# Last expert without products between its pieces, earlier decoding of the first dense columns, another use of a spare buffer: a fused attention, mixture and dense kernel

## The chip, the core and the metric

The kernel runs on one core of one Trainium2 chip. The metric is the time of one execution on the device in microseconds (us); the times below are medians of runs. The trace is of one further, profiled execution. Its engines are TensorE (PE, with its weight loads shown apart as PEld), VectorE (DVE), ScalarE (ACT), GpSimd (POOL) and SyncE (SP); here SP alone issues the loads from and stores to main memory, which 16 DMA engines carry out.

## What is computed

Three layers follow one another on 2304 tokens of width 512 (4 batches of 576; float32, the dense weights come as 64-bit floats):

```python
# attention, 8 heads of 64: heads 0-3 see the 32 latest positions, heads 4-7 every 32nd
attn = softmax(where(mask, scale * q @ k.T, -1e9));  x = attn @ v          # x: 2304 x 512
# mixture: 8 experts with 4 slots each, 512 -> 1024 -> 512
logits = x @ phi                                      # 2304 x 32
slot_input = softmax(logits, axis=0).T @ x            # 32 x 512
h = maximum(slot_input[e] @ w1[e], 0);  slot_out[e] = h @ w2[e]
x = softmax(logits, axis=1) @ slot_out                # 2304 x 512
# dense layer, 512 -> 2048 -> 512
h = x @ w_in;  g = where(h > 0, h, exp(minimum(h, 0)) - 1)
out = g @ w_out
```

## The kernel before

**Stages.** First comes the attention: 20 units (`units`, the loop over `it` at L498), each a head pair `p`, a stretch `t` and a half `h`, in the order of pairs 2, 3, 0, 1. While it runs, the first-layer weights `w1[e]` of the experts are loaded, 2 MB each in four DMAs of 512 KB. Then the column softmax and its product (`acc`, L574) give the 32 slot inputs. `emit_w1(a)` (L658) makes the first expert layer for two experts at a time, `a` from 0 to 3, `emit_w2(e)` (L748) the second layer, eight products for each expert, all added up in one place (`acc`; the variable is `yp`). Each of the eight takes 32 columns of the PE array; the eight go round its four column groups twice. The eight experts' results are 32 rows. Copies (`y_sb`, L800 on ACT and L801 on DVE), products with a 0/1 matrix (L805), the copy `soT` (L807) and products with the dense weight (L883, L894) turn them into a small matrix `M4`, so that the wide product with `w_in` over all tokens is one with `M4` and the row softmax `cT` (L974). From there the dense stage runs: exponential and the like on ACT and DVE, and three products for each 128 tokens and 128 rows of `w_out` (L1016 to L1018), since both sides are split in a high and a low part.

**Decoding.** A dense weight is stored as a 64-bit float. `dec_abs` (L727, ACT) and `dec_1`, `dec_2`, `dec_3` (L731, L735, L741, DVE) turn one block of it into 32-bit floats. The first 256 columns of `w_in` are loaded early as four "heads" of 256 KB, each behind an expert's weight in the spare end of its buffer (`load_head`, L450). Decoded they go to `dec`, which is the buffer half `wb0`. That half holds the second expert's `w2` until that expert's products are done.

**Buffers and loads.** The weights lie in regions that the attention uses first: slot 9 is `kA` (the keys of pairs 2 and 0), slot 7 is `kB` (pairs 3 and 1), slot 5 the queries of pairs 3 and 0, slot 6 the values of pair 0, slots 1, 2 and 4 other regions of the attention. Slot 8 (`ex`) belongs to nothing else. The table `LOADS` (L489) says behind which unit which `w1` is issued into which slot. `load_w` issues a weight; L703 issues the second-layer weights `w2[3]` to `w2[7]` behind `emit_w1(a)`. All loads stand in one row on SP. Each of them waits for the load eight places ahead of it to have landed, and for the last reader of its buffer; what stands behind a waiting load waits with it. Behind the experts come `w_out` for the first blocks (L722, into `wb1`), the other 256 columns of the first `w_in` block (L716, slot 9), and further blocks of both.

**Warm-up products.** `warm(n)` (L411) emits 2n products of a matrix with itself whose result nobody reads. `W6` is how many stand between the pieces of the last expert (L752), `W7` and `W8` those around L805. In the dense stage's first microseconds a planner (L1062 on) works out an order of all remaining instructions from estimated durations; where it expects PE to be idle, it fills in such products (L1111), as many as its estimate gives.

Of the kernel before, what the change touches and what calls it, by code (L numbers as in the profile page):

```python
# [19 lines left out]
def attn_moe_mlp(ctx, tc, q, k, v_l, v_s, phi, w1, w2, w_in, w_out, out):  # L20
# [12 lines left out]
    NEG = -8.0e9  # L33
    SLOT = 4608
    W0, W2, W3, W4, W5 = 8, (0, 0, 0, 0, 0), 0, 0, 0
    W6, W7, W8, W9 = 1, 3, 2, 1
    CO = (2, 3, 0, 1)
    Q0, WC = 4, 4
    HALF = S * B
# [17 lines left out]
    WP, HP = 256, 2  # L57
# [17 lines left out]
    def slot(i, name):  # L75
        if not isinstance(i, int):
            return i
        t = region(SLOT_AT[i], name)
        return t[:, 0:min(SLOT, t.shape[1])]
# [272 lines left out]
    with tc.manual_schedule():  # L352
# [92 lines left out]
        wsl, w_tiles, w64h = {}, {}, []  # L445
# [7 lines left out]
        def load_w(e, second, s, part=None):  # L453
            if (e, second) not in wsl:

                if not isinstance(s, int):
                    t = s
                elif second:
                    t = w_tiles[s]
                else:  # L460
                    t = w_tiles[s] = slot(s, f"w{e}")
                t = t[:, 0:4096]
                wsl[e, second] = t.rearrange("p (c x) -> p c x", c=8 if second else 4)
            t = wsl[e, second]
            src = w2[e].rearrange("c p x -> p c x") if second else w1[e].rearrange("(c p) x -> p c x", p=128)
            if not second:
                for c in range(4):
                    nc.sync.dma_start(out=t[:, c], in_=src[:, c])
                if s in (9, 5, 7):
                    load_head(s)  # L470
                return
            for c in range(0, 8, 2) if part is None else range(part, part + 4, 2):
                nc.sync.dma_start(out=t[:, c:c + 2].rearrange("p c x -> p (c x)"), in_=src[:, c // 2])
# [6 lines left out]
        def qkv(p, kind):  # L480
# [7 lines left out]

        LOADS = {  # L489
            0: ((0, "q"), (0, "v")), 3: ((0, "k"), (0, 0), (1, "q")), 5: ((1, "v"),), 7: ((1, "k"),),  # L490
            9: ((1, 2), (2, 4)), 13: ((3, 9), (4, 5)), 15: ((5, 8), (6, 6)), 19: ((7, 7),),
        }

        nu = len(units)
# [159 lines left out]
        def emit_w1(a):  # L654
            hp = s_ps[a % 2]
            for c in CO:
                for g in range(4):
                    nc.tensor.matmul(  # L658
                        hp[32 * g:32 * g + 32, :], siT[:, c, :], w_at(2 * a + g // 2, 0, 2 * c + g % 2),
                        start=(c == CO[0]), stop=(c == CO[-1]),  # L660
                    )
            hs = small("pt", 512, "hs", 2)
            nc.scalar.activation(out=hs, in_=hp, func=AF.Relu)
            return hs

        def emit_h1T(a, hs):
            ps = ps_t.tile([128, 4, 4, NS], F32, tag="t", name="htps")
            for c in range(4):
                nc.tensor.transpose(
                    ps[:, c].rearrange("p g s -> p (g s)"), hs[:, 128 * c:128 * c + 128], ident  # L670
                )
            for e2 in range(2):
                e = 2 * a + e2
                nc.vector.tensor_copy(
                    out=h1T[e][:, :, SPE * e:SPE * e + SPE].rearrange("p (f c) s -> p f c s", f=2),
                    in_=ps[:, :, 2 * e2:2 * e2 + 2, SPE * e:SPE * e + SPE].rearrange("p c f s -> p f c s"),
                )
# [14 lines left out]
        for a in range(NE // 2):  # L692
            hs = emit_w1(a)
            if a == 0:
                nc.scalar.activation(out=c4[:, :, 0, :].bitcast(F32R), in_=lt, func=AF.Copy)
                nc.vector.tensor_tensor(out=c4[:, :, 2, :], in0=lt, in1=c4[:, :, 0, :], op=ALU.subtract)
                for x in (0, 2):
                    nc.scalar.activation(out=c4[:, :, x + 1, :], in_=c4[:, :, x, :], func=AF.Copy)
            if prev is not None:
                emit_h1T(*prev)  # L700
            prev = (a, hs)
            for e, x in (((3, 0), (4, 2)), ((5, 4),), ((6, 5), (7, 8)), ())[a]:
                load_w(e, 1, x)  # L703

        w64 = {}
# [1 line left out]
        def load_w64(kind, i, s, part=None):  # L707
            if (kind, i) not in w64:
                t = slot(s, f"w64_{kind}_{i}")[:, 0:4096]
                w64[kind, i] = t.rearrange("p (c x a) -> p c x a", c=4, a=2).bitcast(I32)  # L710
            t = w64[kind, i].rearrange("p c x a -> p c (x a)")
            if kind == 0:
                src = w_in[:, 1024 * i:1024 * i + 1024].rearrange("(c p) f -> p c f", p=128)
                if part is not None:
                    t, src = t[:, :, 2 * part[0]:2 * part[1]], src[:, :, 2 * part[0]:2 * part[1]]
                nc.sync.dma_start(out=t, in_=src)  # L716
            else:
                src = w_out[512 * i:512 * i + 512, :].rearrange("(c p) x -> p c x", p=128)
                if part is None:
                    nc.sync.dma_start(out=t, in_=src)  # L720
                else:
                    nc.sync.dma_start(out=t[:, part], in_=src[:, part])  # L722
# [3 lines left out]
        def dec_abs(src, dst):  # L726
            nc.scalar.activation(out=dst, in_=src[:, :, 1].bitcast(F32), func=AF.Abs, scale=ESC)  # L727
# [17 lines left out]
        def emit_w2(e):  # L745
            for c in range(8):
                g = c % 4
                nc.tensor.matmul(  # L748
                    yp[32 * g:32 * g + 32, :], h1T[e][:, c, :], w_at(e, 1, c),
                    start=(e == 0 and c < 4), stop=(e == NE - 1 and c >= 4),  # L750
                )
                if e == NE - 1 and c in (1, 3, 5):  # L752
                    warm(W6)

        pers = slot(6, "pers")
        dec = wb0.rearrange("p (i x) -> p i x", x=512)
# [13 lines left out]
        for e in range(NE - 1):  # L770
            emit_w2(e)
            if e == 1:
                emit_h1T(*prev)
            if e >= 4:
                for i0 in range(6 * (e - 4), 6 * (e - 4) + 6, 3):
                    emit_ct(i0)
        for c in range(4):
            dec_abs(w64h[c], dec[:, c, 0:WP])
        for c in range(4):
            for d_ in (dec_1, dec_2, dec_3):  # L780
                d_(w64h[c], dec[:, c, 0:WP])
        warm(W5)
        emit_w2(NE - 1)
        loads, due = {}, -1.35
# [9 lines left out]
            due += 5.83  # L794
            loads[x] = due
        load_w64(0, 1, 0)
        load_w64(1, 1, 5)

        y_sb = small("pt", DM, "y_sb", 2)
        nc.scalar.activation(out=y_sb[:, 0:256], in_=yp[:, 0:256], func=AF.Copy)  # L800
# [234 lines left out]
        for si, gi, s, f0, f1, y, T in ev_n:  # L1035
# [18 lines left out]
            x = node("V" if f0 else "A", 0.6 if f0 else 0.48, deps, key, f_ev, ("ob", rel) if f1 == NF else None)  # L1054
# [30 lines left out]
        while len(order) < len(nodes):  # L1085
            best = (1e8,)
            for e in free:
                c = [(start_of(n), nodes[n][3], n) for n in ready[e]]
                if c:
                    lim = min(c)[0] + EPS  # L1090
                    x = min((key, t, n) for t, key, n in c if t <= lim)
                    best = min(best, (x[1], x[2], e))
            t, n, e = best
# [72 lines left out]
```

## Time and profile before

| | us |
|---|---|
| median of 3 runs | 378.37 |
| lowest and highest of them | 377.45, 378.55 |
| the profiled execution | 376.64 |
| its span, first to last instruction | 374.9 |

In the span PE is busy 341.6 us (91%), PEld 249.6 us, DVE 255.8 us, ACT 233.9 us, POOL 35.1 us. The span falls into an attention up to some 92 us, a mixture up to some 144 us, and the dense stage from 150.64 us, when the first L1016 starts. The profile gives start, duration and count of instructions in order of time, with the idle time ahead of them and what ended it in brackets; a row can stand for several instructions of one kind. Matmuls overlap, so that the starts of successive rows say more than the durations. The DMA rows give the time from the issue of a load to its landing.

### The profile page before, as it was taken

How to read it: one execution, taken by the hardware profiler on the slowest of the kernel's cores; microseconds unless marked ns; L12 is line 12 of the kernel's file. 1: busy time of each engine (PE TensorE's matmuls, PEld its weight loads, DVE VectorE, ACT ScalarE, POOL GpSimd, SP SyncE). 2: the span in 40 equal slices, each digit the busy share in tenths (PEclk: the TensorE clock that was granted, in tenths of full speed). 3: DMA queues.
4: the chain of work that ended last, by engine and by line, in shares of the span. 5: the costliest groups of instructions: out<-in, count | busy, mean ns of one | idle time of the engine just before them, and what ended most of it. 6: DMA issues, size and time to landing. Idle time of an engine off the chain costs nothing.

```text
span 374.9 us, 8089 instructions
## 1 busy us (share of the span) xinstructions
PE 341.6 (91%) x3287; PEld 249.6 (67%) x3287; DVE 255.8 (68%) x522; ACT 233.9 (62%) x462; POOL 35.1 (9%) x75
## 2 busy tenths in 40 slices
PE   6365988878799999999999999999999999999995
PEld 4344666556233337878688778888868888888884
DVE  6564858658360028979999999999854665476741
ACT  6395865325232046999999678868665666666660
POOL 8401964000020000000000000000000000000000
PEclk9598899989999999999999999999999999999999
DMA  6999999998999989764100144100000011032301
GB/s 205 394 399 392 395 331 366 379 407 319 388 412 406 408 352 379 294 226 166 59 2 0 27 200 169 55 3 0 0 2 0 0 57 57 0 114 112 113 2 57
DMA packets 23606, 71.64 MB, mean 191 GB/s; under 512 B 2192, under 2 KB 2320, under 8 KB 23568
## 3 DMA queue, kind: packets, MB, share of 16 engines
q1 hardware_dynamic: 23568, 71.12, 49.9%
q8 instruction: 26, 0.43, 0.5%
q14 instruction: 12, 0.10, 0.1%
HBM read 66.39 MB, written 4.72 MB: 190 GB/s over the span
## 4 chain that ended last, share of the span: by engine, by line
PE 83%; ACT 6%; DVE 4%; issue 3%; DMA 2%; SPq 0%; ACTq 0%
PE ops L1016 18%; PE ops L1017 17%; PE ops L1018 17%; PE hps L974 4%; PE acc L748 4%; PE s_ps L658 4%; ACT bd L258 2%; DMA kA<-in_k_dram 2%; PE xtps L334 2%; PE s_ps L200 2%; PE lo L292 2%; PE so L316 1%; PE wps L1111 1%; PE acc L574 1%; PE ptps L272 1%
## 5 line engine op out<-in xcount | busy, mean ns | idle before, releaser
L984 DVE SCALAR_TENSOR_TENSOR g<-hps,g 128x512 f32<-128x512 f32 (+1 forms) x80 | 50.6, 632 | 18.2 <-ACT g L981 18.2
L978 ACT ACTIVATE g<-hps 128x512 f32<-128x512 f32 (+1 forms) x80 | 44.2, 552 | 20.6 <-PE hps L974 19.2
L981 ACT ACTIVATE g<-g 128x512 f32<-128x512 f32 (+1 forms) x80 | 46.9, 586 | 1.4
L1018 PE MATMUL ops<-wh,glo 128*128 128x512 f32 x86 | 33.5, 390 | 0.0
L1018 PE MATMUL ops<-w,glo 128*128 128x512 f32 x86 | 33.5, 389 | 0.0
L990 ACT ACTIVATE ghi<-g 128x512 fp32r<-128x512 f32 (+1 forms) x40 | 23.5, 588 | 14.3 <-DVE g L984 12.9
L990 ACT ACTIVATE rings<-g 128x512 fp32r<-128x512 f32 (+1 forms) x40 | 23.4, 586 | 13.2 <-DVE g L984 11.1
L974 PE MATMUL hps<-pers 128*128 128x512 f32 (+1 forms) x80 | 29.3, 372 | 0.0
L1016 PE MATMUL ops<-wh,ghi 128*128 128x512 f32 x72 | 28.9, 401 | 0.0
L1016 PE MATMUL ops<-wh,rings 128*128 128x512 f32 x72 | 28.8, 400 | 0.0
L1016 PE MATMUL ops<-w,ghi 128*128 128x512 f32 x72 | 28.5, 395 | 0.0
L1017 PE MATMUL ops<-wl,ghi 128*128 128x512 f32 x72 | 28.1, 390 | 0.0
L1017 PE MATMUL ops<-w,rings 128*128 128x512 f32 x72 | 28.1, 390 | 0.0
L1016 PE MATMUL ops<-w,rings 128*128 128x512 f32 x72 | 28.1, 390 | 0.0
L1017 PE MATMUL ops<-w,ghi 128*128 128x512 f32 x72 | 28.1, 390 | 0.0
L1017 PE MATMUL ops<-wl,rings 128*128 128x512 f32 x72 | 28.0, 390 | 0.0
L523 POOL COPY v<-v 32x768 f32<-32x768 f32 (+2 forms) x28 | 20.6, 743 | 26.0 <-DMA v<-in_v_l_dram 21.9
L1018 PE MATMUL ops<-wh,rings 128*128 128x512 f32 x58 | 22.6, 390 | 0.0
L731 DVE TENSOR_SCALAR xw<-xw 128x512 int32<-128x512 int32 (+1 forms) x36 | 13.7, 389 | 13.0 <-ACT xw L727 12.9
L1018 PE MATMUL ops<-w,rings 128*128 128x512 f32 x58 | 22.6, 389 | 0.0
L225 DVE TENSOR_REDUCE mx<-s_ps 128x6 f32<-128x384 f32 (+1 forms) x20 | 10.2, 509 | 15.2 <-PE s_ps L214 9.2
L994 DVE TENSOR_TENSOR glo<-g,rings 128x512 fp32r<-128x512 f32 (+1 forms) x24 | 15.2, 632 | 7.2 <-ACT rings L990 5.0
(193 smaller groups left out, 712.3 us busy)
## 6 DMA issues: line engine op xcount, KB each, us to landing
w<-in_moe_w_dram SPq DMA_DIRECT2D x52, 512.0 KB, 9.3
w<-in_moe_w_in_dram SPq DMA_DIRECT2D x3, 2048.0 KB, 8.6
out_dram<-ob SPq DMA_DIRECT2D x18, 256.0 KB, 2.0
v<-in_v_s_dram SPq DMA_DIRECT2D x8, 512.0 KB, 8.7
xw<-in_moe_w_dram SPq DMA_DIRECT2D x8, 512.0 KB, 9.6
xw<-in_moe_w_out_dram SPq DMA_DIRECT2D x2, 2048.0 KB, 7.8
q<-in_q_dram SPq DMA_DIRECT2D x7, 576.0 KB, 9.6
kB<-in_k_dram SPq DMA_DIRECT2D x8, 288.0 KB, 8.8
```

Of the source, the lines that this page charges most:

```text
L523: nc.gpsimd.tensor_copy(out=o, in_=i)
L658: nc.tensor.matmul(hp[32 * g:32 * g + 32, :], siT[:, c, :], w_at(2 * a + g // 2, 0, 2 * c + g % 2), start=(c == CO[0]), stop=(c == CO[-1]),)
L748: nc.tensor.matmul(yp[32 * g:32 * g + 32, :], h1T[e][:, c, :], w_at(e, 1, c), start=(e == 0 and c < 4), stop=(e == NE - 1 and c >= 4),)
L974: nc.tensor.matmul(t["ps"], M4[:, 128 * f:128 * f + 128], cTf[:, t0:t0 + n], start=True, stop=True)
L978: nc.scalar.activation(out=t["g"], in_=t["ps"], func=AF.Exp)
L981: nc.scalar.activation(out=t["g"], in_=t["g"], func=AF.Relu, scale=-1.0, bias=1.0)
L984: nc.vector.scalar_tensor_tensor(out=t["g"], in0=t["ps"], scalar=0.0, in1=t["g"], op0=ALU.max, op1=ALU.subtract)
L990: nc.scalar.activation(out=t["hi"], in_=t["g"], func=AF.Copy)
L994: nc.vector.tensor_tensor(out=t["lo"], in0=t["g"], in1=t["hi"].bitcast(F32), op=ALU.subtract)
L1016: nc.tensor.matmul(o, t["hi"][:, c], hi, start=(f == f0), stop=False)
L1017: nc.tensor.matmul(o, t["hi"][:, c], lo, start=False, stop=False)
L1018: nc.tensor.matmul(o, t["lo"][:, c], hi, start=False, stop=(f == f1 - 1))
```

## The change

Three edits, in their code:

```diff
-    W6, W7, W8, W9 = 1, 3, 2, 1
+    W6, W7, W8, W9 = 0, 3, 2, 1
...
         LOADS = {
             0: ((0, "q"), (0, "v")), 3: ((0, "k"), (0, 0), (1, "q")), 5: ((1, "v"),), 7: ((1, "k"),),
-            9: ((1, 2), (2, 4)), 13: ((3, 9), (4, 5)), 15: ((5, 8), (6, 6)), 19: ((7, 7),),
+            9: ((1, 2), (2, 4), (3, 8)), 13: ((4, 9), (5, 5)), 15: ((6, 6),), 19: ((7, 7),),
...
-            for e, x in (((3, 0), (4, 2)), ((5, 4),), ((6, 5), (7, 8)), ())[a]:
+            for e, x in (((3, 0), (4, 2)), ((5, 4), (6, 8)), ((7, 5),), ())[a]:
                 load_w(e, 1, x)
...
             if e == 1:
                 emit_h1T(*prev)
+                for c in range(4):
+                    dec_abs(w64h[c], dec[:, c, 0:WP])
+                for c in range(4):
+                    for d_ in (dec_1, dec_2, dec_3):
+                        d_(w64h[c], dec[:, c, 0:WP])
             if e >= 4:
                 for i0 in range(6 * (e - 4), 6 * (e - 4) + 6, 3):
                     emit_ct(i0)
-        for c in range(4):
-            dec_abs(w64h[c], dec[:, c, 0:WP])
-        for c in range(4):
-            for d_ in (dec_1, dec_2, dec_3):
-                d_(w64h[c], dec[:, c, 0:WP])
...
-        load_w64(1, 1, 5)
+        load_w64(1, 1, 8)
```

On PE the last expert's products stand like this before (`w_1338` is that expert's `w2`, x2 are two of its eight products; L416 are the warm-up products):

```order
L764 MATMUL ctps<-ident,c_1823 128x128 x6
L748 MATMUL acc<-w_1338,h1T_c 32x512 x2
L416 LDWEIGHTS ident
L416 MATMUL wps<-ident 128x256
L416 LDWEIGHTS ident
L416 MATMUL wps<-ident 128x256
L748 MATMUL acc<-w_1338,h1T_c 32x512 x2
L416 LDWEIGHTS ident
L416 MATMUL wps<-ident 128x256
L416 LDWEIGHTS ident
L416 MATMUL wps<-ident 128x256
L748 MATMUL acc<-w_1338,h1T_c 32x512 x2
```

and like this after, where the buffer is called `w_1200`:

```order
L748 MATMUL acc<-w_901,h1T_b 32x512 x8
L764 MATMUL ctps<-ident,c_1823 128x128 x6
L748 MATMUL acc<-w_906,h1T_b 32x512 x8
L764 MATMUL ctps<-ident,c_1823 128x128 x6
L748 MATMUL acc<-w_1200,h1T_c 32x512 x8
L416 LDWEIGHTS ident
L416 MATMUL wps<-ident 128x256
```

The eight products now stand in one row; six warm-up products are gone, and nothing else on PE has moved.

On ACT, between the ReLU of the first expert layer (L663) and the copy of the result (L800), the four decoding steps (L727) change places with the six copies of the row softmax (L765):

```order
 L663 ACTIVATE hs<-s_ps_91 128x512
 L663 ACTIVATE hs<-s_ps_92 128x512
-L765 ACTIVATE pers<-ctps 128x3x4x32 x6
-L727 ACTIVATE xw<-w_1189 128x256
-L727 ACTIVATE xw<-w_1195 128x256
+L727 ACTIVATE xw<-w_1194 128x256
+L727 ACTIVATE xw<-w_1200 128x256
 L727 ACTIVATE xw<-w_1607 128x256
 L727 ACTIVATE xw<-w1s 128x256
+L765 ACTIVATE pers<-ctps 128x3x4x32 x6
 L800 ACTIVATE y_sb<-acc 128x256
```

On DVE the twelve decoding steps have no instruction between their old place and their new one, so that DVE's row reads as before.

On SP, in the attention's second half, the loads behind the third expert's `w1` (`w_901`) before (`w_1189` is the fourth expert's, in slot 9):

```order
L468 DMA w_901<-in_moe_w_dram 128x1024 [waits DMAHW3_49]
L468 DMA w_1189<-in_moe_w_dram 128x1024 [waits DMAHW4_49,PE_49]
L468 DMA w_1189<-in_moe_w_dram 128x1024 [waits DMAHW5_49]
L468 DMA w_1189<-in_moe_w_dram 128x1024 [waits DMAHW6_49]
L468 DMA w_1189<-in_moe_w_dram 128x1024 [waits DMAHW7_49]
L450 DMA w_1189<-in_moe_w_in_dram 128x512 [waits DMAHW0_49]
```

and after (`w_906` is the fourth expert's, in slot 8; `w_1194` the fifth's, in slot 9):

```order
L468 DMA w_901<-in_moe_w_dram 128x1024 [waits DMAHW3_49]
L468 DMA w_906<-in_moe_w_dram 128x1024 [waits DMAHW4_49]
L468 DMA w_906<-in_moe_w_dram 128x1024 [waits DMAHW5_49]
L468 DMA w_906<-in_moe_w_dram 128x1024 [waits DMAHW6_49]
L468 DMA w_906<-in_moe_w_dram 128x1024 [waits DMAHW7_49]
L468 DMA w_1194<-in_moe_w_dram 128x1024 [waits DMAHW0_49,PE_49]
```

The fourth expert's weight no longer waits for PE, only for the load eight places ahead (the DMAHW names); the wait for PE now stands at the fifth expert's weight, `w_1194`. The number of loads on SP and their order by expert are as before; the two early heads of `w_in` go with the fifth and the sixth expert's weight instead of the fourth and the fifth. The planner's order for the dense stage is the same.

## Rows read from the trace of the kernel before

**Rows 1.** The page: PE's granted clock in 40 slices of the span, in tenths.

```profile
PEclk9598899989999999999999999999999999999999
```

**Rows 2.** Windows: start:end length, busy of each engine, PEclk, DMA share, GB/s.

```profile
150.00:160.00 10.00, 10.00 (x47) 8.11 (x45) 10.00 (x25) 9.99 (x22) 0.00 (x0) 1.00 0.69 273
...
360.00:370.00 10.00, 10.00 (x46) 8.28 (x45) 2.86 (x8) 3.06 (x8) 0.00 (x0) 1.00 0.01 2
```

**Rows 3.** Timeline of PE, seventh and eighth expert to the dense stage.

```profile
134.38 1.92 PE L748 MATMUL acc<-w,h1T_b 128*32 128x512 f32 x16
136.24 0.88 PE L764 MATMUL ctps<-ident,c 128*128 128x128 f32 x6
137.04 1.05 PE L748 MATMUL acc<-w,h1T_c 128*32 128x512 f32 x4
...
140.96 1.05 PE L748 MATMUL acc<-w,h1T_c 128*32 128x512 f32 x4
141.95 0.83 PE L416 MATMUL wps<-ident 128*128 128x256 bf16 x6
...
150.64 0.48 PE L1016 MATMUL ops<-wh,rings 128*128 128x512 f32 x1
```

**Rows 4.** Timeline of SP's issues, and each one's KB and us to landing.

```profile
127.46 0.33 SPq L473 DMA_DIRECT2D w<-in_moe_w_dram  x1
...
128.75 0.33 SPq L473 DMA_DIRECT2D w<-in_moe_w_dram  x1
...
w<-in_moe_w_dram SPq DMA_DIRECT2D x1, 512.0 KB, 10.2
...
130.07 0.33 SPq L722 DMA_DIRECT2D xw<-in_moe_w_out_dram  x1
...
xw<-in_moe_w_out_dram SPq DMA_DIRECT2D x1, 512.0 KB, 10.1
...
139.32 0.38 SPq L716 DMA_DIRECT2D w<-in_moe_w_in_dram  x1
```

**Rows 5.** Windows, as in rows 2: the load stream full, and its gaps.

```profile
62.00:64.00 2.00, 1.81 (x66) 1.34 (x55) 1.61 (x5) 1.14 (x3) 0.00 (x0) 1.00 0.65 219
86.00:87.00 1.00, 1.00 (x60) 0.69 (x50) 0.92 (x4) 0.13 (x1) 0.00 (x0) 1.00 0.52 197
130.00:135.00 5.00, 5.00 (x48) 2.07 (x44) 0.00 (x0) 1.71 (x4) 0.00 (x0) 1.00 1.02 406
```

**Rows 6.** SP's longest wait between 80 and 95 us, and the issue behind it.

```profile
SPq L468 <- PE lg L341: 7.8, 1, 7.8
...
86.55 1.02 SPq L468 DMA_DIRECT2D w<-in_moe_w_dram  x2
```

**Rows 7.** Timeline of ACT and DVE around the decoding and behind it.

```profile
131.55 0.87 ACT L765 ACTIVATE pers<-ctps 128x384 fp32r<-128x384 f32 x2 [9.87 <-PE ctps L764]
...
142.12 0.39 ACT L800 ACTIVATE y_sb<-acc 128x256 f32<-128x256 f32 x1 [3.13 <-PE acc L748]
142.40 0.67 ACT L727 ACTIVATE xw<-xw 128x512 f32<-128x512 f32 x1
...
138.05 0.29 DVE L731 TENSOR_SCALAR xw<-xw 128x256 int32<-128x256 int32 x1 [12.02 <-ACT xw L727]
...
142.54 0.42 DVE L801 COPY y_sb<-acc 128x256 f32<-128x256 f32 x1
```

**Rows 8.** Timeline of PE at two stops, windows behind and between, the code queue.

```profile
15.48 0.76 PE L214 MATMUL s_ps<-kA,q 128*18 128x36 f32 x37 [6.02 <-DMA kA<-in_k_dram]
...
77.91 0.30 PE L292 MATMUL lo<-v,lpt 64*32 64x64 f32 x3 [2.31 <-issue]
...
78.00:82.00 4.00, 4.00 (x87) 2.70 (x87) 2.48 (x7) 0.49 (x1) 0.00 (x0) 0.57 1.03 411
100.00:102.00 2.00, 1.06 (x6) 0.14 (x4) 0.76 (x2) 0.31 (x1) 0.00 (x0) 1.00 1.03 411
...
q8 instruction: 26, 0.43, 0.5%
```

## The prediction

> **What bounds the kernel now.** I read the timeline of PE from the end. From the first L1016 at 150.64 us on, each stretch of 10 us up to 370 us shows PE busy for all of it at the full clock, 2.4 GHz; the first and the last of these 22 windows stand for the others [rows 2]. So whatever moves the start of the dense stage moves the end by as much, and nothing in this change touches the stage itself. That start ends a chain: the last expert's products, the copy `y_sb`, L805, `soT`, `M4`, the first L974, and then work in which DVE and ACT take turns. The question is how early the last expert's products can end. Two things can hold them: PE's own row [rows 3] and the landing of that expert's `w2` [rows 4]. For the landing I read the load stream: between 130 and 135 us it moves 406 GB/s with the DMA engines busy throughout [rows 5], and each load of 512 KB lands 10.2 us after its issue [rows 4], which is eight loads at 1.28 us (127.46 to 128.75), the depth of SP's row. The stream is full there, and its last piece sets a floor.
>
> **Part 1, no warm-up products between the pieces.** Before, four pieces of two products start from 137.04 to 140.96, 1.31 us apart, and the products behind them at 141.95 [rows 3]: 4.91 us. A piece without the warm-up takes 0.98 us (140.96 to 141.95), so three pairs of warm-up products cost 0.33 each, 1.0 us in all. The larger part lies elsewhere: two products use half of the array's columns. The expert before, with its eight in one row, takes 134.38 to 136.24, 1.86 us [rows 3]. By PE alone the last expert would go from 137.04 to 138.90, 3.05 us earlier.
>
> But the data are not there. The last piece is issued at 128.75 and lands 10.2 us later, at 138.95 [rows 4]. The third lands at 127.46 + 10.2 = 137.66, the first two 1.28 us apart before that, at 135.1 and 136.4. So after the change the first four products run from 137.04 to about 137.9, the next two to about 138.9, and the last two begin at about 139.0 instead of 140.96. From there all is as before: the last piece takes its 0.98 us, and ACT's copy follows. **Minus 1.95 us**, with minus 3.05 as the far end if the data came earlier.
>
> What is late next? ACT's copy `y_sb` goes from 142.12 to 140.2, and the first block of `w_out` is wanted behind it, at 142.40 [rows 7], then 140.45. It is issued at 130.07 and lands 10.1 us later, at 140.2 [rows 4]. That just holds, and if it did not, the decoding on DVE stands behind `soT` anyway, so that a few tenths more would cost nothing. PE waits about 0.1 us for the last two products, which no longer hide a landing.
>
> **Part 2, the decoding moved.** Four ACT steps (each less than the 0.67 us of the L727 on 512 columns at 142.40, so under 2.7 us) and twelve DVE steps (4.5 us, from 138.05 to the copy at 142.54) move to behind the second expert's products. There they lie under idle time: ACT waits 9.87 us up to 131.55, so from 121.7 on, and DVE 12.02 us up to 138.05, so from 126.0 on [rows 7]. Even begun at 126.0 they end by 128.7 and some 131. If that cover were gone they would hold back the copies of the row softmax at 131.55 by at most their 2.7 us. Does the free DVE help? Its half of `y_sb` starts 0.42 us behind ACT's (142.54 against 142.12) because of the decoding. But L805 takes its four products in order, and the first two need ACT's half alone; the gain is between 0 and 0.4, and I take **0**.
>
> The other consequence is on SP. The half of the first `w_in` block (L716) waits for the readers of slot 9, the first head among them, so before it is issued only at 139.32 and the three loads behind it wait too [rows 4]. Now it can go at about 132.6, when the load eight places ahead has landed. It and what follows land earlier or at the same time, and all of it is used later than it lands now, too. **0** here. The price from above: were these loads to share the engines with the last expert's pieces instead of following them, 1 MB at 406 GB/s is 2.6 us, and part 1 would be lost. The expert's pieces and the `w_out` behind them land 10.2 and 10.1 us after their issue [rows 4]: loads land in the order of issue, at the stream's pace, whatever stands behind them.
>
> **Part 3, the spare buffer.** The fourth expert's `w1` no longer waits for the keys in slot 9. That closes the gap at 62 to 64 us: 2 x (406 - 219) GB/s is 0.37 MB, 0.92 us of stream [rows 5]. I expect it to be handed back. The eighth expert's `w1` waits for PE's last reader of slot 7, 7.8 us long, and is issued at about 86.5 [rows 6]; the stream runs dry just then, 197 GB/s between 86 and 87 [rows 5]. Finishing 0.92 us sooner only makes this wait and gap longer, since PE's progress in the attention decides. From there to the last expert's `w2` the bytes, the order and the waits are the same, so the floor at 138.95 stays. **0**, with minus 0.92 as the far end (the floor falls to 138.0, the saving grows to 2.9). The seventh expert's `w2` in slot 8 may also be issued one `emit_w1` earlier, but it stands in a full stream that waits for landings, not for buffers: 0.
>
> **Sum.** The profiled execution takes 376.64 us, a span of 374.9 and 1.74 around it; 376.64 - 1.95 = 374.7. The median of the runs is 378.37, 1.73 above that execution. On its level the forecast is 378.37 - 1.95 = **376.4 us**, 0.5% less.
>
> **The rivals.** (a) *The floor falls too.* If the filled gap is not handed back, the last pieces land at 138.0 or before, and PE's row bounds: 2.9 to 3.05 us, 375.4. For it: 0.92 us really is lost at 62 to 64. Against: the wait of 7.8 us in rows 6. 12%.
>
> (b) *The next wait takes the gain.* `w_out` lands later than 140.2 behind a deeper row of loads, or the loads freed from the wait share the engines after all. From 1 us of delay on, half of the gain or more is gone: 377.8. Against: the order of landing in rows 4. 14%.
>
> (c) *Slower: a longer code stop in the attention.* At 77.91 PE has stood for 2.31 us in the middle of a row of like products (L292), released by nothing that the profile shows; a code queue with 26 packets runs beside the loads [rows 8]. Behind the stop the granted clock is 0.57 over 78 to 82, so 1.2 GHz for 3.4 of the 4 us [rows 8]. The gap at 62 to 64, in which code could pass, is now filled. One more such stop costs 2.3 us, and 3.4 us at half clock behind it 1.7: 376.4 + 4.0 = 380.4. It decides from 3.1 us on, since less leaves the forecast under the bound of a slowdown. Against: the stop stands beside a full stream already, so a full stream elsewhere is nothing new, and a stop can vanish as well. 9%. The Trainium skill ("Runtime: NRT & Kernel Launch", Instruction fetch mechanics) says that the sequencer fetches the next page while it executes the current one, the cost being mostly hidden. By that the rival's price is nothing and the time 376.4; the 2.31 us at 77.91 do not look hidden, though no row ties them to the code queue.
>
> (d) *Slower: the clock.* The removed products may have held TensorE's clock. It fell to 1.2 GHz for the whole second slice of the span, 9.4 us [rows 1], in a stretch where PE stood 6.02 us [rows 8]. As long a fall at the last expert would cost half its length, 4.7 us: 381.1. It must last over 6.2 us to end slower. Against: at 100 to 102 PE was busy 1.06 of 2 us and the clock stayed [rows 8], and here PE would stand for 0.1 us. 4%. The Trainium skill ("TensorE: Matmul & The Clock Gate", HAM oscillation) speaks against the change: short bursts of products with waits for data between them bring the clock down again and again. By that rule (d) would be likely; rows 8 show such a stretch without a fall.
>
> **How the numbers follow.** The forecast holds 61%, (a) 12, (b) 14, (c) 9, (d) 4. The range takes the forecast and (a), the half gain of (b), and some shift of stops either way: 374.9 to 378.4. A change under 0.3%, 1.1 us, can't be told from none in this kernel. Faster by more: nearly all of the forecast's cases and (a), 0.72. Within: (b) and some of the forecast's, 0.19. Slower: 0.09, most of (c) and (d) beyond their deciding points.
>
> **What would show it.** Right: in the profile after, the last expert's L748 begins at about 137.0, its last products at about 139.0, `y_sb` on ACT at 140.2, L1016 at 148.7; L727 of the heads before 128; the stream without a gap at 62 to 64 and with a longer one before 88; the clock at full behind 137. Wrong: the last pieces landing before 138 (a), an idle ACT or DVE waiting for `w_out` before 150 (b), a last expert that starts well behind 137.04 because the attention ended later (c), or a clock below full behind 137 (d).

## The result, and the profile after

| | before | after |
|---|---|---|
| median of 4 runs each, in alternation (us) | 378.46 | 374.77 |
| lowest and highest (us) | 377.45, 379.93 | 373.19, 375.18 |
| the profiled execution (us) | 376.64 | 373.19 |
| its span (us) | 374.9 | 371.4 |

The ratio is 0.9897, with a 95% interval of 0.9855 to 0.9939. The forecast was 376.4 us with a range of 374.9 to 378.4: the kernel did get faster, but by more than forecast, and the measured median lies 0.13 us below the range. The experiments further down give 43 more runs with parts 1 and 2 of the change (19 of them with all three parts) and 94 more runs of the kernel before.

The time went where the forecast looked for it, in the last expert. The timeline of PE in the kernel after (start, duration, engine, line and operation, the count, and in brackets the idle time ahead and what ended it) has these rows in place of rows 3:

```profile
133.90 1.92 PE L748 MATMUL acc<-w,h1T_b 128*32 128x512 f32 x16
135.75 0.88 PE L764 MATMUL ctps<-ident,c 128*128 128x128 f32 x6
136.56 2.40 PE L748 MATMUL acc<-w,h1T_c 128*32 128x512 f32 x16
138.90 0.83 PE L416 MATMUL wps<-ident 128*128 128x256 bf16 x6
...
147.59 0.48 PE L1016 MATMUL ops<-wh,rings 128*128 128x512 f32 x1
```

The four pieces are one row now. From its first product to the row behind it the last expert takes 138.90 - 136.56 = 2.34 us, where it took 4.91. The expert ahead of it takes 135.75 - 133.90 = 1.85 us for the same products, so some 0.5 us of waiting is left. Where it lies is seen at the weight loads of the same products (engine PEld):

```profile
137.44 0.12 PEld L748 LDWEIGHTS acc<-w,h1T_c 128*32 128x32 f32 x2 [0.31 <-issue]
137.91 0.14 PEld L748 LDWEIGHTS acc<-w,h1T_c 128*32 128x32 f32 x4 [0.35 <-DMA w<-in_moe_w_dram]
```

On SP stand the issue of the last piece of that weight, its size and its time to landing, and the issue of the `w_in` half (L716):

```profile
127.59 0.33 SPq L473 DMA_DIRECT2D w<-in_moe_w_dram  x1
...
w<-in_moe_w_dram SPq DMA_DIRECT2D x1, 512.0 KB, 10.3
...
131.47 0.38 SPq L716 DMA_DIRECT2D w<-in_moe_w_in_dram  x1
```

127.59 + 10.3 is 137.9, and at 137.91 the last two products' weight loads begin, released by that DMA. So the landing is the floor, as forecast, but it lies at 137.9 instead of 138.95. That is before 138, which the prediction named as the sign of its rival (a); whether the buffers did it is a question for the experiments.

The first L1016 moves from 150.64 to 147.59, by 3.05 us. Of these 4.91 - 2.34 = 2.57 come from the last expert and 137.04 - 136.56 = 0.48 from its earlier start. From the first L1016 to the last product of the program it is 219.41 us in both. The tail behind the last product is shorter by 0.45 (4.85 before, 4.40 after). The sum, 2.57 + 0.48 + 0.45, is 3.50, the difference of the spans. The 0.48 and the 0.45 lie where the change has no instruction, and the experiments show both to vary from one execution to the next.

Behind the last expert ACT and DVE look like this (rows 7 are those of before). The first two rows are the decoding of the heads, far ahead of everything that waits for it:

```profile
123.79 1.11 ACT L727 ACTIVATE xw<-w 128x256 f32<-128x256 f32 x3 [2.59 <-PE acc L748]
124.81 0.42 ACT L727 ACTIVATE xw<-w1s 128x256 f32<-128x256 f32 x1
...
139.07 0.38 ACT L800 ACTIVATE y_sb<-acc 128x256 f32<-128x256 f32 x1 [1.86 <-PE acc L748]
139.35 0.66 ACT L727 ACTIVATE xw<-xw 128x512 f32<-128x512 f32 x1
...
139.49 0.42 DVE L801 COPY y_sb<-acc 128x256 f32<-128x256 f32 x1 [9.46 <-ACT y_sb L800]
```

DVE's half of `y_sb` still begins 0.42 us behind ACT's, though DVE has been idle for 9.46 us: what releases it is ACT's half, not the decoding.

The load stream (windows: start:end, length, busy time of each engine, PE's clock, share of the DMA engines, GB/s; these answer to rows 5):

```profile
62.00:64.00 2.00, 1.26 (x54) 1.07 (x53) 1.63 (x5) 1.28 (x3) 0.00 (x0) 1.00 1.04 412
84.00:86.00 2.00, 1.55 (x58) 1.19 (x62) 0.84 (x2) 0.64 (x2) 0.00 (x0) 1.00 0.18 66
86.00:88.00 2.00, 1.80 (x79) 1.27 (x70) 1.88 (x6) 0.38 (x2) 0.00 (x0) 1.00 0.43 33
130.00:135.00 5.00, 5.00 (x48) 2.12 (x44) 0.03 (x1) 1.74 (x4) 0.00 (x0) 1.00 1.02 404
```

The gap at 62 to 64 is closed, 412 GB/s for 219. At 84 to 88 the stream now stands almost still. In the kernel before the same two windows are these:

```profile
84.00:86.00 2.00, 2.00 (x71) 1.48 (x73) 1.68 (x4) 1.65 (x4) 0.00 (x0) 1.00 1.01 401
86.00:88.00 2.00, 1.73 (x77) 1.21 (x67) 1.85 (x6) 0.38 (x2) 0.00 (x0) 1.00 0.69 141
```

SP's wait ahead of that (line, what it waits for: us in total, times, longest) and the issue behind it show why; rows 6 have 7.8 us and 86.55:

```profile
SPq L468 <- PE lg L341: 11.4, 2, 9.4
...
86.62 1.76 SPq L468 DMA_DIRECT2D w<-in_moe_w_dram  x4
```

The wait for the last reader of slot 7 (the longest of the two) has grown from 7.8 to 9.4 us and, in this pair of traces, ends at the same time. The loads came earlier and then waited longer.

### The profile page after: what moved, and what is told of

Read it like the earlier page. It is cut to its first block, busy times and chain, and to the rows that moved or that the text cites. A ratio compares the mean times of both kernels' runs of the same rounds, so it can differ in the third digit from the quotient of the medians.

```text
span 371.4 us, 8079 instructions
## 1 busy us (share of the span) xinstructions
PE 339.4 (91%) x3281; PEld 249.6 (67%) x3281; DVE 256.3 (69%) x522; ACT 234.3 (63%) x462; POOL 35.1 (9%) x75
## 4 chain that ended last, share of the span: by engine, by line
PE 84%; DVE 5%; ACT 4%; issue 3%; DMA 3%; ACTq 0%
PE ops L1016 18%; PE ops L1017 18%; PE ops L1018 18%; PE hps L974 5%; PE acc L748 4%; PE s_ps L658 4%; DMA kA<-in_k_dram 3%; PE s_ps L200 2%; PE xtps L334 2%; ACT bd L258 2%; PE lo L292 2%; PE so L316 1%; PE wps L1111 1%; PE ptps L272 1%; PE acc L574 1%
## 5 line engine op out<-in xcount | busy, mean ns | idle before, releaser
L1016 PE MATMUL ops<-wh,ghi 128*128 128x512 f32 x72 | 28.9, 401 | 0.0
L1016 PE MATMUL ops<-wh,rings 128*128 128x512 f32 x72 | 28.8, 400 | 0.0
L1016 PE MATMUL ops<-w,ghi 128*128 128x512 f32 x72 | 28.5, 395 | 0.0
L1016 PE MATMUL ops<-w,rings 128*128 128x512 f32 x72 | 28.1, 390 | 0.0
L994 DVE TENSOR_TENSOR glo<-g,ghi 128x512 fp32r<-128x512 f32 (+1 forms) x24 | 15.2, 634 | 5.0 <-ACT ghi L990 3.1
```

The costliest lines, as they stand in the source:

```text
L994: nc.vector.tensor_tensor(out=t["lo"], in0=t["g"], in1=t["hi"].bitcast(F32), op=ALU.subtract)
L1016: nc.tensor.matmul(o, t["hi"][:, c], hi, start=(f == f0), stop=False)
```

## Experiments

All were timed in five rounds. Kernels of one group ran on one chip with their own runs of the kernel before: 35 of them for the first four, 29 for the next four, 30 for the last four. Together these are 94 runs of before, with a median of 376.97 us, the lowest 374.34, the highest 379.89. Beside the ratio, which comes from all runs, each kernel has a number from its one trace that I call the **last stretch**: from the last expert's first product to the first L1016. It is 13.60 us in the kernel before (137.04 to 150.64) and 11.03 after (136.56 to 147.59).

| kernel | what it has | median, us (runs) | ratio to before, 95% | last stretch, us | last piece lands after the expert's start, us |
|---|---|---|---|---|---|
| before | - | 376.97 (94) | 1 | 13.60 | 1.91 |
| after, first comparison | all | 374.77 (4) | 0.9897 (0.9855 to 0.9939) | 11.03 | 1.34 |
| e1_warm | part 1 | 378.05 (12) | 1.0026 (1.0004 to 1.0047) | 15.14 | 1.46 |
| e2_slot | part 3 | 376.95 (12) | 0.9997 (0.9981 to 1.0014) | 13.60 | 1.8 |
| e3_decode | part 2 | 377.04 (12) | 0.9994 (0.9976 to 1.0012) | 13.60 | 1.7 |
| e4_warm_slot | parts 1 and 3 | 378.49 (12) | 1.0033 (1.0004 to 1.0062) | 13.61 | 1.88 |
| e5_warm_decode | parts 1 and 2 | 375.06 (12) | 0.9950 (0.9921 to 0.9979) | 11.06 | 1.36 |
| e6_all | all | 374.36 (12) | 0.9937 (0.9908 to 0.9966) | 11.62 | 1.88 |
| e7_head6 | all, a head elsewhere | 374.55 (12) | 0.9937 (0.9909 to 0.9966) | 10.75 | 1.1 |
| e8_landed | all, no wait for the last weight | 373.27 (6) | 0.9892 (0.9855 to 0.9930) | 10.56 | - |
| e9_extra | all, one more load ahead | 376.51 (12) | 0.9991 (0.9967 to 1.0015) | 11.89 | 2.25 |
| e10_all | all | 374.39 (7) | 0.9927 (0.9900 to 0.9953) | 11.80 | 2.05 |
| e11_warm_decode | parts 1 and 2 | 374.75 (12) | 0.9946 (0.9923 to 0.9969) | 13.02 | 3.3 |
| e12_head6 | all, a head elsewhere | 375.07 (12) | 0.9933 (0.9912 to 0.9954) | 11.11 | 1.4 |

The expectations name three theories. A: the last piece's landing sets the end of the last expert, the decoding on DVE would hold the copy of the result if it stayed in its place, and the buffer edit makes the stream land earlier. B: what the first comparison gave beyond minus 1.95 us is the spread of the runs, and neither the decoding nor the buffers have a part in it. C: the warm-up products were the whole cost. The experiments bear out A on the landing and on the decoding, and B on the buffers and the spread; C fails at the first one.

### Part 1 alone

```diff
-    W6, W7, W8, W9 = 1, 3, 2, 1
+    W6, W7, W8, W9 = 0, 3, 2, 1
```

> Only the warm-up products between the last expert's pieces are gone (W6 = 0); decoding and buffers as before. Theory A (landing and cover): DVE still decodes the heads from 138.05 to 142.54, ahead of its half of y_sb, so the result's copy cannot end earlier than before although PE is done by about 140: 0 to -0.3 us against before, L1016 at 150.4 to 150.7. Theory C (the warm-ups were the whole cost): -2 to -3 us. Theory B (the spread of the runs explains what went beyond -1.95 us) says -1.95 here too, since it gives the decoding no part.

Measured: 1.0026 (1.0004 to 1.0047), slower by about 1 us. B's and C's gain is not there, and A did not foresee the loss. The timeline of PE in that kernel:

```profile
137.34 2.55 PE L748 MATMUL acc<-w,h1T_c 128*32 128x512 f32 x16
139.83 0.83 PE L416 MATMUL wps<-ident 128*128 128x256 bf16 x6
140.49 0.58 PE L805 MATMUL s_ps<-e,y_sb 128*128 128x32 f32 x4
143.33 1.02 PE L805 MATMUL s_ps<-e,y_sb 128*128 128x32 f32 x4 [2.26 <-DVE y_sb L801]
...
152.48 0.48 PE L1016 MATMUL ops<-wh,rings 128*128 128x512 f32 x1
```

The first and the last of the decoding steps on DVE, and the copy behind them:

```profile
138.36 0.29 DVE L731 TENSOR_SCALAR xw<-xw 128x256 int32<-128x256 int32 x1 [12.03 <-ACT xw L727]
...
142.51 0.42 DVE L741 SCALAR_TENSOR_TENSOR xw<-w1s,xw 128x256 int32<-128x256 int32 x1
142.85 0.42 DVE L801 COPY y_sb<-acc 128x256 f32<-128x256 f32 x1
```

And the windows around PE's wait (the clock is the third number from the end):

```profile
142.00:144.00 2.00, 0.67 (x4) 0.68 (x5) 1.20 (x4) 0.00 (x0) 0.00 (x0) 0.85 1.03 383
144.00:146.00 2.00, 2.00 (x22) 1.19 (x21) 1.32 (x3) 0.10 (x1) 0.00 (x0) 0.50 1.05 422
146.00:148.00 2.00, 2.00 (x18) 1.60 (x15) 0.36 (x2) 1.13 (x5) 0.00 (x0) 0.80 1.02 418
```

The last expert does end early here, in 139.83 - 137.34 = 2.49 us. Then PE waits 2.26 us for DVE's half of `y_sb`, which stands behind the twelve decoding steps. Those begin only behind ACT's decoding step, which stands behind the copies of the row softmax. They end at 142.85, 5.51 us after the expert's start. In the kernel before they end at 142.54, 5.50 us after its start: the decoding ended at the very moment at which ACT's half of `y_sb` was done. It was a second floor, level with the row of pieces.

And behind this wait the granted clock is 0.50 over 144 to 146, 1.2 GHz, with 0.85 and 0.80 in the windows around it. From the second half of L805 to L1016 it is 152.48 - 143.33 = 9.15 us, where the kernel below without such a fall takes 7.62. The 1.53 between them are what the last stretch has lost against before (15.14 - 13.60 = 1.54). The Trainium skill ("TensorE: Matmul & The Clock Gate", HAM oscillation) says that waits for data between short bursts of products bring the clock down again and again. This row, with its fall to 0.50 behind one wait, agrees with it; the row of e4 below, with a wait of 1.77 us, shows no fall.

### Part 3 alone, and part 2 alone

```diff
-            9: ((1, 2), (2, 4)), 13: ((3, 9), (4, 5)), 15: ((5, 8), (6, 6)), 19: ((7, 7),),
+            9: ((1, 2), (2, 4), (3, 8)), 13: ((4, 9), (5, 5)), 15: ((6, 6),), 19: ((7, 7),),
...
-        load_w64(1, 1, 5)
+        load_w64(1, 1, 8)
```

> Only the spare buffer: the fourth expert's w1 into slot 8 and the buffers behind it as in the changed kernel; warm-ups and decoding as before. Theory A: the gap at 62 to 64 us is closed and the last expert's last piece lands near 138.0 instead of 138.95, but PE's row with the warm-ups (1.31 us a piece) does not use it: 0 to -0.5 us, the latter if the attention ends half a microsecond earlier as in the changed kernel's trace. Theory B: landing as before at 138.9, and 0 us. A theory that the buffer alone brings the gain beyond -1.95 would see -1 to -1.7 us.

Measured: 0.9997 (0.9981 to 1.0014), and a last stretch of 13.60, that of before. The landing that A forecast near 138.0, about 1 us behind the expert's start, is not there: it lies 1.8 us behind it, where it lay 1.91.

For part 2 the loops over `dec_abs`, `dec_1`, `dec_2` and `dec_3` move as in the change, and nothing else.

> Only the decoding of the heads moved behind the second expert. Theory A: 0 us (within 0.4), since PE's row with the warm-ups holds the result to 142.0; DVE's half of y_sb starts at 142.1 instead of 142.54, and the load of the rest of the first w_in block goes out at about 132.6 instead of 139.3. Theory B: 0 as well. If the decoding were on the path by itself: -0.4 us.

Measured: 0.9994 (0.9976 to 1.0012), again 13.60. DVE, free of the decoding, copies its half here at the same distance from the expert's start (143.18 - 137.68 = 5.50), and waits for ACT's half:

```profile
143.18 0.42 DVE L801 COPY y_sb<-acc 128x256 f32<-128x256 f32 x1 [12.02 <-ACT y_sb L800]
```

So of two floors that were level, parts 1 and 2 take away one each. Alone neither gives a gain.

### Part 1 with part 3, part 1 with part 2, and all three

> Warm-ups gone and the spare buffer, decoding as before. Theory A: DVE's decoding up to about 142 holds the result again: 0 to -0.7 us against before. Theories B and C: -2 to -3 us.

Measured: 1.0033 (1.0004 to 1.0062), slower, where A expected 0 to a small gain. The timeline of PE:

```profile
143.61 0.63 PE L805 MATMUL s_ps<-e,y_sb 128*128 128x32 f32 x4 [1.77 <-DVE y_sb L801]
...
151.23 0.48 PE L1016 MATMUL ops<-wh,rings 128*128 128x512 f32 x1
```

The window behind the wait:

```profile
143.00:145.00 2.00, 1.39 (x24) 1.14 (x24) 1.24 (x5) 0.00 (x0) 0.00 (x0) 1.00 1.07 401
```

The wait for the decoding is there as in e1 (DVE's half at 143.13, 5.51 behind the expert's start), but 1.77 us long, and in this execution the clock stayed at full: 151.23 - 143.61 = 7.62 us, a last stretch of 13.61, neither gain nor loss. The profiled execution took 376.79 us and the median 378.49. That the clock falls in others of its executions would explain the difference, but only this one was traced.

> Warm-ups gone and decoding moved, buffers as before. Theory A: the last piece lands at about 138.95 as before and holds the last two products: -1.95 us (-1.5 to -2.4), y_sb on ACT at 140.2. Theory B (what went beyond -1.95 is spread of the runs): the same as the full change in the same rounds, so either both near -2 or both near -3.5. Theory C: -3 us.

> The full change again, in five rounds. Theory A: -3.0 to -3.7 us, 1.0 to 1.7 more than with the buffers as before. Theory B: -1.9 to -2.4, no more than with the buffers as before.

Measured: 0.9950 (0.9921 to 0.9979) without the buffers, 0.9937 (0.9908 to 0.9966) with them. The last expert on PE's timeline, first without the buffer edit (e5):

```profile
137.94 2.45 PE L748 MATMUL acc<-w,h1T_c 128*32 128x512 f32 x16
140.32 0.83 PE L416 MATMUL wps<-ident 128*128 128x256 bf16 x6
```

and then with it (e6):

```profile
139.12 3.01 PE L748 MATMUL acc<-w,h1T_c 128*32 128x512 f32 x16
142.06 0.83 PE L416 MATMUL wps<-ident 128*128 128x256 bf16 x6
```

2.38 and 2.94 us: in these two executions the kernel *with* the buffer edit waits longer for the landing. That the buffers bring the landing forward, as A had it, with 1.0 to 1.7 us more gain, finds nothing here, nor in e2.

Both were run once more on another chip:

> Warm-ups gone and decoding moved, buffers as before, once more. Theory A: -1.9 to -2.6 us against before and within 0.5 us of the full change, since the spare buffer's earlier load is handed back at slot 7. If the spare buffer carries part of the gain: 1 us or more behind the full change.

> The full change once more, to see how much of the first comparison is the spread of runs. Theory A with the spread: -2.0 to -2.6 us against before, the median of twelve runs within 0.6 us of 374.4. If the first comparison's -3.7 is the size of the change: -3 to -4 us.

Measured: 0.9946 (0.9923 to 0.9969) and 0.9927 (0.9900 to 0.9953). The 19 runs of all three parts have a median of 374.39, the 24 of parts 1 and 2 one of 374.88. The 0.5 us between them lie in the same direction on both chips, but the intervals overlap widely; whether the buffers give anything at all stays open. PE's timeline in e11 shows how far the landing can slip:

```profile
138.79 1.83 PE L748 MATMUL acc<-w,h1T_c 128*32 128x512 f32 x8
140.84 1.05 PE L748 MATMUL acc<-w,h1T_c 128*32 128x512 f32 x4 [0.22 <-DMA w<-in_moe_w_dram]
142.15 1.05 PE L748 MATMUL acc<-w,h1T_c 128*32 128x512 f32 x4 [0.26 <-DMA w<-in_moe_w_dram]
143.13 0.83 PE L416 MATMUL wps<-ident 128*128 128x256 bf16 x6
```

Here two pieces are waited for, 1.31 us apart, about the 1.28 us of stream that 512 KB take, and the last stretch is 13.02.

### Is the landing the floor?

First the floor taken away: the last expert's products read the weight of the expert before, which has long landed. This changes what is computed, so the time is that of a kernel that does not wait for the last weight.

```diff
-                    yp[32 * g:32 * g + 32, :], h1T[e][:, c, :], w_at(e, 1, c),
+                    yp[32 * g:32 * g + 32, :], h1T[e][:, c, :], w_at(min(e, NE - 2), 1, c),
```

> The full change, but the last expert's second-layer products read the weight of the expert before it, which has landed earlier; the last expert's own weight is still loaded and left unread, so the output is not the reference's. Theory A: no wait for the last piece, 1.86 us instead of 2.34 for the eight products: -0.5 us against the full change, and no more, since PE's own row is the next bound. If the landing no longer mattered in the changed kernel: 0.

The last expert on PE's timeline:

```profile
136.68 1.92 PE L748 MATMUL acc<-w,h1T_c 128*32 128x512 f32 x16
138.54 0.83 PE L416 MATMUL wps<-ident 128*128 128x256 bf16 x6
```

Measured: 1.86 us for the last expert, a last stretch of 10.56, which is 3.04 less than before. The far end of the prediction, by PE alone, was 3.05. The time is 0.9892 (0.9855 to 0.9930), 1.1 us below that of e6 beside it; the last stretches differ by 1.06. The expectation of 0.5 came from the trace after alone, whose landing was early; against the three traces of the full change (11.03, 11.62 and 11.80) the last stretch is shorter by 0.47 to 1.24. So the landing still costs the full change between half a microsecond and a little over one, and without it the last expert takes no longer than the ones ahead of it.

Then the floor raised, by a load of 512 KB that nobody reads, ahead of the last expert's weight:

```diff
+                if e == 7:
+                    nc.sync.dma_start(out=w_tiles[9][:, 0:1024], in_=w2[7, 0])
```

> The full change, and one more load of 512 KB (a piece of w2 into the dead buffer of the fifth expert's w1, read by nobody) ahead of the last expert's weight. Theory A (the landing of the last piece holds the result): the last pieces land 1.28 us later against the start of the last expert, and the stretch from that start to the first L1016 grows by as much, from 11.0 to 11.6 us to 12.3 to 12.9; the time grows by about 1.3 us against the full change. If PE's row held the result, the stretch stays at 11.0 to 11.6 and the time does not change.

The same place (lines are shifted by two):

```profile
139.15 1.99 PE L750 MATMUL acc<-w,h1T_c 128*32 128x512 f32 x12
141.37 1.05 PE L750 MATMUL acc<-w,h1T_c 128*32 128x512 f32 x4 [0.23 <-DMA w<-in_moe_w_dram]
142.35 0.83 PE L416 MATMUL wps<-ident 128*128 128x256 bf16 x6
```

Measured: 376.51 us, 2.1 more than e10 beside it, and PE waits for the landing. The direction fits, the size in this trace doesn't: the last piece lands 2.25 us behind the expert's start, 0.2 to 0.9 later than in the three traces of the full change and not 1.28, and the last stretch is 11.89. Much of the reason can be read off the traces. Counted from SP's issue behind the wait at slot 7, the piece lands 53.0 us later (88.39 to 141.4), beside 51.3, 51.8 and 51.9 in the traces of the full change, so it did come 1.1 to 1.7 us later. But in this execution PE was late too: it stopped for 1.12 us in L574, released by nothing that the profile shows, and from L574 to L658 it took 12.05 us, for 11.1 to 11.2. Of the 2.1 us between the medians the landing would give 1.28, which the two intervals allow; where the rest comes from isn't shown.

The table holds the strongest evidence for the floor, and it spans more than any one experiment. Eight traces have the decoding moved and a landing to wait for: after, e5, e6, e7, e9, e10, e11 and e12. In them the landing behind the expert's start runs from 1.1 to 3.3 us and the last stretch from 10.75 to 13.02, and the second minus the first is always 9.64 to 9.75 us. The prediction's own sum says the same: 13.60 - 1.95 - 1.91 = 9.74. Below the 10.56 of e8, by PE alone, an earlier landing can't shorten it.

### A try at bringing the landing forward

The third head goes with the seventh expert's weight instead of the eighth's, out of the row behind the wait at 86 us:

```diff
-                if s in (9, 5, 7):
+                if s in (9, 5, 6):
```

> The full change, and the third head of w_in (256 KB) loaded behind the seventh expert's w1 in slot 6 instead of behind the eighth's in slot 7, so ahead of the gap at 84 to 88 us in which the stream stands, not behind it. Theory A: the bytes between that gap and the last expert's last piece shrink by 256 KB, 0.63 us of stream; the piece lands at about 137.2, PE's last expert runs in about 1.86 us instead of 2.34: -0.4 to -0.5 us against the full change. A theory that the floor is not the byte stream but SP's waits (places of the issues) sees no change of the landing.

> The full change with the third head in slot 6, ahead of the gap, once more: 0.3 to 0.6 us below the full change by theory A, the last piece landing 1.1 us or less behind the start of the last expert; no difference if the places of the issues and not the bytes set the landing.

Measured: 0.9937 (0.9909 to 0.9966) and 0.9933 (0.9912 to 0.9954), beside 0.9937 and 0.9927 of the full change. The last pieces land 1.1 and 1.4 us behind the expert's start and the last stretches, 10.75 and 11.11, are at the short end, but the times do not show the 0.3 to 0.6 us that were expected of it, and their intervals are too wide to deny them. No version was found that clearly beats the full change.

## Why the prediction came out as it did

**What bounds the kernel: right.** The chain through the last expert to the first L1016 was the place, the dense stage behind it took the same 219.41 us, and the last piece's landing ends the wait in the trace after, at 137.91. e8 takes the landing away and gets the 3.04 us that PE alone was to give.

**Part 1: right mechanism, a term taken as fixed that varies.** The minus 1.95 us came from one landing, 1.91 us behind the expert's start. In the other traces that have a landing to wait for (e9 with its added load apart), the same difference runs from 1.1 to 2.05 us, and once it is 3.3. Hence the last stretch of the full change is shorter by 2.57, 1.98 and 1.80 us in three traces; e6, whose landing is 1.88, gives the 1.98 almost as forecast. In two groups of runs the medians fell by 2.6 us (376.93 to 374.36 and 376.96 to 374.39). That is 0.6 more than 1.95, but 1.95 (a ratio of 0.9948) lies inside both intervals, so that the term was too small is likely and not shown.

**Part 2: the price was right for the wrong reason, and the sum was not a sum.** The prediction put DVE's 0.42 us down to the decoding and so gave the move 0. The 0.42 are a wait for ACT's half. What the decoding did in the kernel before was to end exactly with the copy, 5.50 us after the last expert's start (142.54 - 137.04) [rows 3, 7]. Moving it alone gives 0.9994; leaving it in place turns part 1 from a gain of about 2 us into a loss of 1. The prediction moved ACT's copy forward to 140.2 and did not ask where DVE's row of 4.5 us, ending at 142.54, would then be had it stayed. The total wasn't touched by this, since all three parts were made; the split was wrong, since the gain needs both parts. Its other consequence came as said: L716 is issued at 131.47 (132.6 forecast), and nothing came of it.

**Part 3: right in its 0, not in every step.** The gap closed, the wait at slot 7 grew, and e2 stands at 0.9997. The end of that wait stayed in the trace after (86.62 for 86.55), but not in general: SP's issue behind it comes between 86.19 and 89.18 us in the nine traces with the buffer edit and between 86.51 and 87.18 in the five without. Under (c) it is seen where that goes.

**The level: the step that failed.** "On its level the forecast is 378.37 - 1.95 = 376.4 us." The three runs given had a median of 378.37. Over 94 runs the kernel before takes 376.97, with 374.34 to 379.89 between its ends. Of the 1.6 us between the forecast and the 374.77 measured, this level makes 1.4 (378.37 - 376.97). The profiled execution, 376.64, was close to the median of the 94, and the sum on its basis, 374.7, is 0.3 us from the 374.39 of 19 runs; that this one execution lay there and not elsewhere between the ends was luck. I had both levels and took the one with three runs behind it, all within 1.1 us, which looked tighter than the kernel is. The range was made from causes alone, and gave that spread only a phrase ("some shift of stops either way"). The first comparison's minus 3.7 us is for the same reason more than the change is worth: its four runs of before are those three and one more, and their 378.46 lies 1.5 us above the 94, while the four runs after lie only 0.4 above the 19. Within that comparison the level held and the miss shows as too large a change; it is the 94 runs that tell the two apart. Why the first runs of before lay so high isn't shown. The profiled pair is 3.5 us apart because that execution after began its last expert 0.48 us early, had an early landing and a tail 0.45 us short.

**The rivals.** (a) The floor falls because of the filled gap: its sign came, a landing at 137.9, but not by its cause. Landings behind the expert's start vary as much without the buffer edit (1.36 to 3.3) as with it (1.34 to 2.05, all heads in place). (b) The next wait: ACT waits for PE alone at 139.07, and goes on at 139.35 with the block that rows 7 show at 142.40; not seen. (c) A longer code stop: it came, but no cost of it shows. The stops that nothing in the profile releases are longer in the trace after, 6.4 us in sum between 55 and 92 against 4.5 before. The longest on PE's timeline, against rows 8:

```profile
65.47 0.49 PE L272 MATMUL ptps<-ident,ls 128*128 128x128 f32 x3 [2.21 <-issue]
...
78.18 0.30 PE L292 MATMUL lo<-v,lpt 64*32 64x64 f32 x3 [2.58 <-issue]
...
84.45 0.68 PE L292 MATMUL lo<-v,lpt 64*32 64x64 f32 x42 [1.08 <-issue]
```

The windows behind two of them:

```profile
66.00:70.00 4.00, 4.00 (x88) 2.86 (x87) 1.38 (x3) 1.83 (x4) 0.00 (x0) 0.59 1.03 410
78.00:82.00 4.00, 3.82 (x111) 2.81 (x115) 3.36 (x9) 1.32 (x3) 0.00 (x0) 1.00 1.05 413
```

The clock fell behind the stop at 65.47 instead of the one at 77.91, and the next stage (L574) starts at 93.86 us for 93.79, so that the stops took the place of other waiting. All traces together show more: the stop at 65 to 68 us is 2.19 to 2.48 us long in all nine with the buffer edit, and there it is at most 1.38 in the five without (one of these, e11, has 2.67 at 72.73). Behind SP's issue at slot 7, up to 92 us, the longest stop is 0.41 in the nine and 0.76 to 2.55 in the five. e5, without the buffer edit, beside the rows above:

```profile
65.05 0.49 PE L272 MATMUL ptps<-ident,ls 128*128 128x128 f32 x3 [1.11 <-issue]
...
90.29 0.70 PE L272 MATMUL ptps<-ident,ls 128*128 128x128 f32 x5 [2.55 <-issue]
```

Beside this last stop the stream of e5 moves 340 GB/s (88 to 90 us). So where the filled gap was, PE now stands longer, and where the stream now stands still, it stands less: from SP's issue to L574 it is 7.23 or 7.24 us in the nine and 7.24 to 9.13 in the five. That it is code which PE waits for isn't shown. Over all traces L574 starts at 94.94 us on the mean in the nine with the buffer edit and at 94.86 in the five without it: no loss and no gain shows there.

(d) The clock: with all three parts it stays at full behind the last expert. With part 1 alone it fell, behind a wait of 2.26 us that the decoding made, so this rival was real, and moving the decoding, which takes that wait away, is what kept it off.

## What to carry to other kernels

Before a wait is removed, ask of *every* engine that the next step needs when its row would be done if it stayed as it is: two floors can end at the same moment, and then each edit alone shows nothing, or a loss, and the pair shows the gain. A transfer that lands just as it is needed is not one number but a spread, here of a microsecond and once of two, and the gain inherits it. And neither one execution nor three runs fix the level of a forecast: three runs that agreed to 0.3% did not show a spread of 1.5%, and the range has to take that spread in.

## What the runs showed of the hardware

Runs of the same kernel lie up to 5.5 us apart (374.34 to 379.89 for the kernel before). The traces show three places for it: the products of L574 begin anywhere from 93.43 to 96.42 us, after an attention with stops of 0.2 to 2.7 us (between 55 and 92) that nothing in the profile releases and, in all traces but one (e9), a fall of the clock that comes behind one of them or another; from there to L658 it is between 10.5 and 12.1 us; and the tail behind the last product takes 4.3 to 4.9 us. From L658 to the last expert it is 31.47 or 31.48 us in all traces but one (32.03, e11, where the seventh expert waits for its weight too), and from the first L1016 to the last product 219.41 to 219.44 in all. The stops at 65 to 68 and at 88 to 91 us are long beside a running load stream and short or gone where it pauses, as told under (c); no run tests whether the stream causes them. What does, and why the last piece lands 1.1 us behind the expert's start in one execution and 3.3 in another, was not tried and stays open.

One wait of PE of 2.26 us was followed by 1.2 GHz, and one of 1.77 us at the same place in the program was not (e1 and e4).
